# Packed attention and two feed-forward stages on one core: the product with v and the second scores at 128 columns, and one small tile padded to 256 bytes

## The chip, the cores and the metric

The kernel runs on one core of a Trainium2 chip. The metric is the device time of one execution in microseconds (us), and the time before is the median of three executions. One more execution was taken with the hardware profiler; its rows are what the text reads.

## The reference, cut to what matters

```python
p_packed = sm_attn(p, k, v)          # 32 packed queries per head: softmax(p k^T / 8) v
out = sm_attn(q, p_packed, p_packed) # softmax(q p_packed^T / 8) p_packed
x = out as (2304, 512)               # 4 blocks of 576 tokens, 8 heads of 64
x = relu(x @ w_in)**2 @ w_out        # 512 -> 2048 -> 512, weights in float64
logits = x @ w_gate                  # 8 experts; exp, then 8 rounds of row and column balancing give P
out = sum_e P[:, e] * (relu(x @ w1[e]) @ w2[e])   # 512 -> 1024 -> 512
```

## The kernel before, in words

**Attention.** The four blocks b are worked one after the other. Heads go in pairs j = 0..3, a pair filling the 128 partitions (64 each). `scores1(b)` (L191) makes the first scores and their softmax, 128 rows being four heads' 32 packed queries. `pack(b)` (L212) transposes them (`tr`, L219, L224), and multiplies them with v (`pp`, L232): for a pair j and a piece c of the 576 tokens (four of 128, one of 64) the stationary operand is 128 columns of v, the moving one 64 columns of the transposed softmax. Only the two diagonal 64x32 blocks of each 128x64 result are wanted; they are copied into the zeroed tile `bd` (L235 to L238, VectorE the upper half of the partitions, ScalarE the lower). `bd` is also split into two fp32r parts in `BDP` (L243, L244). `scores2(b)` (L250) multiplies 128 tokens of q (stationary) with the 64 columns of `bd` of a pair (`s`, L260), each pair into 64 columns of its own, and takes the softmax on VectorE and ScalarE (L266 to L273). `attn_T` (L276) transposes it (`trc`, `trd`) into `at`.

All these products are in float32. A float32 matmul that is no transpose is issued as two instructions, each with its own weight load, so 20 products of a block are 40 instructions.

**The first feed-forward stage** is built of `g_unit` (L314), which multiplies `BDP` with w_in (L320) and splits the result into the tiles `g` (ACT L329, DVE L330); `h1_unit` (L342), `at` times `g` (L350); and `x2_unit` (L362, L369). Their weights come as float64 words: each piece passes ACT, DVE `cb` (L111) and `cc` (L113), POOL (L114), ACT (L148) and POOL (L149) into a tile `w`, one piece after the other through one buffer `cc`.

**The second feed-forward stage.** Tokens form three groups p of 768, 512 and 1024 tokens (tiles of 384, 256 and 512 columns). `unit(n, p)` (L668) runs seven products of six matmuls each (`product`, L612, matmul L620): stationary are 128 columns of a `w1` tile, moving is a tile `xc` of x. Between the products stand the second matmuls `y_unit` of the unit before (L646: stationary `hh`, moving a `w2` tile). Groups 0 and 1 alternate for n = 0..31; group 2 follows alone for n = 31..62.

**Where the tiles lie.** SBUF tiles come from pools stacked from the left and from the right. The pool `gp` (L500) is opened on the left when attention ends; `xpb`, `wpb`, `gb`, `xca`, `xcb` and `xcc` are opened on top of it. `both` (L503) is `[2 * E, LINE]` floats, 128 bytes in a partition. With it, the tiles of `wpb`, `gb`, `xca`, `xcb`, `xcc` and group 2's `acc` start at 0 modulo 256 bytes in their partition; those of `wpa`, `xc1`, `xcd`, `ta`, `hp` and all of attention's start at 128 modulo 256. A split weight goes to `wpb` if its number k has k % 12 >= 8 (L146, L147), which makes it so that for even n the four `w1` tiles lie in `wpb`, and for odd n in `wpa`; the `w2` tiles lie in `wpa` always. Of group 2's operands B11, B21 and T1 (products A11, A12, S1) lie in `xcc`, the other four (S2, S4, S3, A22) in `ta` and `xcd`.

**The order of work.** The kernel is written block by block, and a scheduler orders the instructions of each engine from that; each engine then works through its own list in order. SP issues the DMAs in order too.

Of the kernel before, what the change touches and what calls it, by code (L numbers as in the profile page):

```python
# [10 lines left out]
F32 = mybir.dt.float32  # L11
F32R = mybir.dt.float32r
I32, U32, I64 = mybir.dt.int32, mybir.dt.uint32, mybir.dt.int64
AF = mybir.ActivationFunctionType
# [7 lines left out]
E, F = 8, 1024  # L22
NJ = H // 2
# [11 lines left out]
LINE = 32  # L35
# [3 lines left out]
def kernel(ctx: ExitStack, tc: tile.TileContext, qT, kT, v, pT,  # L39
                                     win, wout, wg, w1, w2, out):  # L40
    nc = tc.nc

    def open_pool(name, **kw):
        st = ExitStack()
        return st, st.enter_context(tc.tile_pool(name=name, bufs=1, reuse_waits="tile", **kw))

    def pool(name, **kw):
        st, p = open_pool(name, **kw)
        ctx.push(st)
        return p  # L50
# [11 lines left out]
    stA, pa = open_pool("pa", side="left")  # L62
    ps_attn = {}
# [94 lines left out]
    KQ, V = {}, {}  # L158
# [53 lines left out]
    def pack(b, En):  # L212
        vt = V[b]
        ETs = []
        for g in range(2):
            et = pa.tile([128, 5, 128], F32, tag="et", name="et", bufs=2)
            ps = ps_attn["now"].tile([128, 4, 128], F32, tag="tr", name="tr", bufs=3)
            for c in range(4):
                nc.tensor.transpose(ps[:, c, :], En[g][:, c * 128:(c + 1) * 128], ident)  # L219
            nc.scalar.activation(et[:, 0:4, :], ps, AF.Copy)  # L220
            ETs.append(et)
        ps = ps_attn["now"].tile([128, 4, 128], F32, tag="tr", name="tr", bufs=3)
        for g in range(2):
            nc.tensor.transpose(ps[:64, g, :], En[g][:, 512:576], ident)  # L224
        nc.scalar.activation(ETs[0][:64, 4, :], ps[:64, 0, :], AF.Copy)
        nc.scalar.activation(ETs[1][:64, 4, :], ps[:64, 1, :], AF.Copy)
        ps = ps_attn["now"].tile([128, NJ, 64], F32, tag="tr", name="pp", bufs=3)
        for j in range(NJ):
            for c in range(5):
                k = 128 if c < 4 else 64  # L230
                o = j % 2 * 64
                nc.tensor.matmul(ps[:, j, :], vt[:k, c, j * 128:(j + 1) * 128], ETs[j // 2][:k, c, o:o + 64],  # L232
                                 start=(c == 0), stop=(c == 4))

        bd = pa.tile([128, NJ, 64], F32, tag="bd", name="bd", bufs=2)  # L235
        nc.gpsimd.memset(bd, 0.0)
        nc.vector.tensor_copy(bd[0:64, :, 0:32], ps[0:64, :, 0:32])
        nc.scalar.activation(bd[64:128, :, 32:64], ps[64:128, :, 32:64], AF.Copy)  # L238
        bp = BDP[b // 2]
        for par in range(2):  # L240
            o = (par ^ (b % 2)) * 64
            hi, lo, src = bp[:, 0, par::2, o:o + 64], bp[:, 1, par::2, o:o + 64], bd[:, par::2, :]
            nc.scalar.activation(hi, src, AF.Copy)  # L243
            nc.vector.tensor_tensor(lo, src, hi.bitcast(F32), op=ALU.subtract)  # L244
        return bd
# [4 lines left out]
    def scores2(b, bd):  # L250
        a2 = pa.tile([128, 5, H, NP], F32, tag="a2", name="a2", bufs=2)
        for t0 in (0, 2, 4):
            nt = min(2, 5 - t0)
            ps = ps_attn["now"].tile([128, 2, 256], F32, tag="tr", name="s2", bufs=3)
            for t in range(nt):
                o = TOFF[t0 + t]
                for g in range(2):
                    for jj in range(2):
                        at = g * 128 + (jj ^ (b % 2)) * 64
                        nc.tensor.matmul(ps[:, t, at:at + 64], KQ["qt", b, g][:, jj, o:o + 128],  # L260
                                         bd[:, 2 * g + jj, :], start=True, stop=True)
            n = nt * H
            psv = ps[:, :nt, :].rearrange("p t (h c) -> p (t h) c", c=NP)
            a = a2[:, t0:t0 + nt, :, :].rearrange("p t h c -> p (t h) c")
            mx = pa.tile([128, 2 * H, 1], F32, tag="mx2", name="mx2", bufs=2)[:, :n, :]
            nc.vector.tensor_reduce(mx, psv, axis=AX.X, op=ALU.max)  # L266
            nc.vector.tensor_tensor(a, psv, mx.to_broadcast([128, n, NP]), op=ALU.subtract)
            nc.scalar.activation(a, a, AF.Exp, scale=1.0 / np.sqrt(D).item())
            sm = pa.tile([128, 2 * H, 1], F32, tag="sm2", name="sm2", bufs=2)[:, :n, :]
            nc.vector.tensor_reduce(sm, a, axis=AX.X, op=ALU.add)  # L270
            nc.vector.tensor_scalar_add(sm, sm, EPS)
            nc.vector.reciprocal(sm, sm)
            nc.vector.tensor_tensor(a, a, sm.to_broadcast([128, n, NP]), op=ALU.mult)  # L273
        return a2.rearrange("p t h c -> p t (h c)")
# [182 lines left out]
    e0 = scores1(0)  # L457
    e1 = scores1(1)
    bd0 = pack(0, e0)
    load_kq("qt", qT, 1)  # L460
    split_w(2)
    load_kq("kt", kT, 2)
    a0 = scores2(0, bd0)
    bd1 = pack(1, e1)
    load_v(2)
    split_w(2)
# [13 lines left out]
    load_kq("qt", qT, 2)  # L480
    load_kq("kt", kT, 3)
    a1 = scores2(1, bd1)
    e2 = scores1(2)
    moe1(0)
    load_v(3)
    attn_T(1, a1)
    bd2 = pack(2, e2)
    moe1(1)
    load_kq("qt", qT, 3)
    e3 = scores1(3)  # L490
    a2 = scores2(2, bd2)
    bd3 = pack(3, e3)
    attn_T(2, a2)
# [6 lines left out]
    gp = pool("gp", side="left")  # L500
    wgr = gp.tile([128, 4, E], F32, name="wgr")
    wgs = gp.tile([128, 4, 128], F32R, name="wgs")
    both = gp.tile([2 * E, LINE], F32, name="both")[:, :E]  # L503
    nc.vector.tensor_tensor(both, ident[:2 * E, 0:E], ident[:2 * E, E:2 * E], op=ALU.add)
    P = gp.tile([128, 160], F32, name="P")[:, :NT * E].rearrange("p (t e) -> p t e", e=E)
    xpb = pool("xpb", side="left")
# [212 lines left out]
    for n in range(NQ):  # L719
        for p in ROUNDS[0]:  # L720
# [8 lines left out]
            else:  # L729
                k = 2 if p == 0 else 1  # L730
# [60 lines left out]
```

## Time and profile before

| | |
|---|---|
| median of 3 runs | 1968.72 us (1968.06 to 1970.12) |
| the profiled execution | 1963.5 us, span 1961.7 us |
| PE (TensorE) busy | 1940.9 us, 99% |
| PEld (weight loads) busy | 1719.0 us, 88% |
| DVE, ACT, POOL busy | 57%, 41%, 39% |
| chain that ended last | PE 93%, DVE 4% |
| TensorE clock granted | 0.7 of full in the first fortieth of the span, 0.8 in the second, 0.9 or more after |

PE is TensorE's matmuls, PEld its weight loads, DVE VectorE, ACT ScalarE, POOL GpSimd. A row of the timeline gives start, length, engine, line, output<-inputs and the count of merged instructions; in square brackets stands the idle time before it and what ended it. Matmuls overlap, so the spacing of two matmuls is read from starts and not from their length. [...]

### The profile page before, as it was taken

Reading aid. Unit: us, or ns where it says so; the run is one execution under the profiler, and the core shown is the slowest. Engines: PE = TensorE matmul, PEld = TensorE weight load, DVE = VectorE, ACT = ScalarE, POOL = GpSimd, SP = SyncE. Lnnn points to the kernel's source line nnn. Section 1 sums busy time; section 2 is a strip of 40 time slices with the busy share of each in tenths; the row PEclk is TensorE's granted clock in tenths of the full one; section 3 lists DMA queues with packets and bytes.
Section 4 is the critical chain, followed back from the end, with each engine's and each line's share of the span. In section 5 each row is a group of like instructions: output and inputs, shape, how many; then the busy total and the mean of one; then the engine's idle time right before and its main releaser. Section 6 shows DMA issues by size and latency. Waiting matters only on the chain.

```text
span 1961.7 us, 27023 instructions
## 1 busy us (share of the span) xinstructions
PE 1940.9 (99%) x10492; PEld 1719.0 (88%) x10492; DVE 1125.4 (57%) x1959; ACT 806.9 (41%) x1702; POOL 769.5 (39%) x753
## 2 busy tenths in 40 slices
PE   9999999998999999999999999999999999999999
PEld 7899999998989899899999899988888888888887
DVE  4667877655755555555555555663554555555555
ACT  5658654645343333333333333344333333333331
POOL 2204312434433333334334343433544455444550
PEclk7899999999999999999999999999999999999999
DMA  7302201000111101111110110121111111111111
GB/s 262 135 28 87 87 30 36 23 1 33 44 44 44 35 32 43 44 44 43 44 43 33 44 43 34 42 78 52 58 50 43 43 65 54 54 44 43 55 53 43
DMA packets 30496, 103.72 MB, mean 53 GB/s; under 512 B 3360, under 2 KB 3360, under 8 KB 30368
## 3 DMA queue, kind: packets, MB, share of 16 engines
q1 hardware_dynamic: 30368, 102.00, 15.2%
q8 instruction: 82, 1.34, 0.3%
q14 instruction: 46, 0.38, 0.1%
HBM read 97.27 MB, written 4.72 MB: 52 GB/s over the span
## 4 chain that ended last, share of the span: by engine, by line
PE 93%; DVE 4%; ACT 1%; POOL 1%; issue 1%; DMA 0%; SPq 0%; POOLq 0%; ACTq 0%; DVEq 0%
PE psy L646 41%; PE psc L620 36%; PE psy L369 8%; PE psh L350 4%; PE pp L232 1%; DVE h L359 1%; PE s L260 1%; PE psh L320 1%; DVE g L330 1%; PE s L199 1%; DVE cc L113 0%; POOL w L149 0%; POOL cc L114 0%; DVE cb L111 0%; DMA kt<-kT 0%
## 5 line engine op out<-in xcount | busy, mean ns | idle before, releaser
L646 PE MATMUL psy<-w,hh 128*128 128x512 f32 x3456 | 870.5, 392 | 0.0
L646 PEld LDWEIGHTS psy<-w,hh 128*128 128x128 f32 x3456 | 634.0, 188 | 120.8 <-DVE acc L664 1.2
L620 PE MATMUL psc<-xc,w 128*128 128x512 f32 (+2 forms) x3456 | 680.8, 338 | 2.8 <-ACT s L691 2.4
L664 DVE SCALAR_TENSOR_TENSOR acc<-psy,P,acc 128x512 f32<-128x512 f32 x528 | 395.2, 749 | 452.7 <-PE psy L646 449.0
L620 PEld LDWEIGHTS psc<-xc,w 128*128 128x128 f32 x3456 | 577.6, 189 | 80.4 <-ACT s L691 2.6
L149 POOL TENSOR_TENSOR w<-raw,w 128x512 fp32r<-128x512 f32 (+1 forms) x252 | 297.0, 1184 | 449.8 <-ACT w L148 448.3
L148 ACT ACTIVATE w<-raw 128x512 fp32r<-128x512 f32 (+1 forms) x252 | 143.5, 575 | 339.4 <-PE psc L620 206.0
L149 POOL TENSOR_TENSOR w<-wt,w 128x512 fp32r<-128x512 f32 x126 | 163.3, 1303 | 290.6 <-ACT w L148 281.8
L369 PE MATMUL psy<-h,w 128*128 128x288 f32 x1536 | 231.2, 297 | 1.2 <-DVE h L359 0.9
L369 PEld LDWEIGHTS psy<-h,w 128*128 128x128 f32 x1536 | 212.1, 188 | 3.5 <-DVE h L359 2.6
L627 DVE SCALAR_TENSOR_TENSOR hh<-psc,hh 128x256 fp32r<-128x256 f32 (+2 forms) x288 | 154.7, 548 | 23.5 <-ACT hh L626 23.3
L626 ACT ACTIVATE hh<-psc 128x256 fp32r<-128x256 f32 (+2 forms) x288 | 139.5, 485 | 40.6 <-PE psy L646 31.2
L350 PE MATMUL psh<-at,g 128*128 128x288 f32 x768 | 127.1, 298 | 4.5 <-DVE g L330 4.5
L627 DVE SCALAR_TENSOR_TENSOR hh<-s,hh 128x384 fp32r<-128x384 f32 (+1 forms) x96 | 89.9, 936 | 67.9 <-ACT hh L626 67.8
L148 ACT ACTIVATE w<-wt 128x512 fp32r<-128x512 f32 x126 | 79.0, 627 | 110.2 <-PE psc L620 93.1
L350 PEld LDWEIGHTS psh<-at,g 128*128 128x128 f32 x768 | 111.0, 189 | 6.6 <-issue 5.1
L620 PE MATMUL psc<-xt,w 128*128 128x384 f32 x576 | 115.0, 338 | 0.0
L682 ACT ACTIVATE s<-psc 128x384 f32<-128x384 f32 (+1 forms) x96 | 46.7, 488 | 165.3 <-PE psc L620 165.3
L620 PEld LDWEIGHTS psc<-xt,w 128*128 128x128 f32 x576 | 102.5, 188 | 3.4
L125 POOL TENSOR_TENSOR wt<-raw 128x256 f32<-128x256 f32 x63 | 47.3, 750 | 123.1 <-DMA raw<-w 122.2
L626 ACT ACTIVATE hh<-s 128x384 fp32r<-128x384 f32 (+1 forms) x96 | 50.3, 524 | 108.0 <-PE psy L646 107.2
L149 POOL TENSOR_TENSOR w<-cc,w 128x512 fp32r<-128x512 f32 x32 | 41.8, 1307 | 119.2 <-ACT w L148 87.3
(114 smaller groups left out, 1454.3 us busy)
## 6 DMA issues: line engine op xcount, KB each, us to landing
raw<-w SPq DMA_DIRECT2D x126, 512.0 KB, 3.6
raw<-win SPq DMA_DIRECT2D x16, 512.0 KB, 3.8
raw<-wout SPq DMA_DIRECT2D x16, 512.0 KB, 3.8
kt<-kT SPq DMA_DIRECT2D x8, 576.0 KB, 5.8
qt<-qT SPq DMA_DIRECT2D x8, 576.0 KB, 8.6
out<-acc SPq DMA_DIRECT2D x18, 256.0 KB, 2.0
vt<-v SPq DMA_DIRECT2D x4, 1024.0 KB, 9.0
vt<-v SPq DMA_DIRECT2D x4, 128.0 KB, 9.2
```

The source lines that it names most:

```text
L125: nc.gpsimd.tensor_tensor(s1, a21, a22, op=ALU.add)
L148: nc.scalar.activation(w[:, 0, :n], t, AF.Copy)
L149: nc.gpsimd.tensor_tensor(w[:, 1, :n], t, w[:, 0, :n].bitcast(F32), op=ALU.subtract)
L199: nc.tensor.matmul(ps[:, u, :CT], bq[:, 2 * g + jj, :], kt[:, jj, u * CT:(u + 1) * CT], start=(jj == 0), stop=(jj == 1))
L350: nc.tensor.matmul(ps, gw[:, x, m * 128:(m + 1) * 128], at[:, y, g, o:o + CT], start=(i == 0), stop=(i == 5))
L369: nc.tensor.matmul(ps, w[:, x, d * 128:(d + 1) * 128], h[:, y, :], start=(i == 0), stop=(i == 11))
L620: nc.tensor.matmul(ps[:, :N], w[:, u, o + k * 128:o + (k + 1) * 128], x[v][:, k, :], start=(start and k + u + v == 0), stop=(k == 1 and u ...
L626: nc.scalar.activation(h[:, 0, :], src, AF.Relu)
L627: nc.vector.scalar_tensor_tensor(h[:, 1, :], src, 0.0, h[:, 0, :].bitcast(F32), op0=ALU.max, op1=ALU.subtract)
L646: nc.tensor.matmul(ps, h[:, x, o * 128:(o + 1) * 128], w[:, y, :], start=(i == 0), stop=(i == 5))
L664: nc.vector.scalar_tensor_tensor(a, ps, P[:, tt, e:e + 1], a, op0=ALU.mult, op1=ALU.add)
L682: nc.scalar.activation(s12[:, 0, :], X[:, :N], AF.Copy)
```

## The change

The product with v takes all 128 columns of the transposed softmax (two pairs of heads) instead of 64, and `pp` and `bd` are 128 columns wide for a pair. A pair's two wanted blocks are copied to the 64 columns of `bd` that are its own in the second scores, the other 64 stay zero. The second scores multiply with these 128 columns and add the two pairs of a group in PSUM (start at the first, stop at the second), where each pair had 64 columns of its own. The number of matmuls does not change. The copies into `bd` are two on each engine instead of one, half as large. `both` becomes 256 bytes wide, so every tile opened after it on the left lies 128 bytes further: all of `wpb`, `gb`, `xca`, `xcb`, `xcc` now start at 128 modulo 256, as the others do; `P` goes from 128 to 0.

```diff
-        ps = ps_attn["now"].tile([128, NJ, 64], F32, tag="tr", name="pp", bufs=3)
+        ps = ps_attn["now"].tile([128, NJ, 128], F32, tag="tr", name="pp", bufs=3)
...
-                o = j % 2 * 64
-                nc.tensor.matmul(ps[:, j, :], vt[:k, c, j * 128:(j + 1) * 128], ETs[j // 2][:k, c, o:o + 64],
+                nc.tensor.matmul(ps[:, j, :], vt[:k, c, j * 128:(j + 1) * 128], ETs[j // 2][:k, c, :],
...
-        bd = pa.tile([128, NJ, 64], F32, tag="bd", name="bd", bufs=2)
+        bd = pa.tile([128, NJ, 128], F32, tag="bd", name="bd", bufs=2)
         nc.gpsimd.memset(bd, 0.0)
-        nc.vector.tensor_copy(bd[0:64, :, 0:32], ps[0:64, :, 0:32])
-        nc.scalar.activation(bd[64:128, :, 32:64], ps[64:128, :, 32:64], AF.Copy)
+        for par in range(2):
+            pos = par ^ (b % 2)
+            for h2 in range(2):
+                u = bd[h2 * 64:(h2 + 1) * 64, par::2, pos * 64 + h2 * 32:pos * 64 + h2 * 32 + 32]
+                w = ps[h2 * 64:(h2 + 1) * 64, par::2, par * 64 + h2 * 32:par * 64 + h2 * 32 + 32]
+                if h2 == 0:
+                    nc.vector.tensor_copy(u, w)
+                else:
+                    nc.scalar.activation(u, w, AF.Copy)
...
-                        at = g * 128 + (jj ^ (b % 2)) * 64
-                        nc.tensor.matmul(ps[:, t, at:at + 64], KQ["qt", b, g][:, jj, o:o + 128],
-                                         bd[:, 2 * g + jj, :], start=True, stop=True)
+                        nc.tensor.matmul(ps[:, t, g * 128:(g + 1) * 128], KQ["qt", b, g][:, jj, o:o + 128],
+                                         bd[:, 2 * g + jj, :], start=(jj == 0), stop=(jj == 1))
...
-    both = gp.tile([2 * E, LINE], F32, name="both")[:, :E]
+    both = gp.tile([2 * E, 2 * LINE], F32, name="both")[:, :E]
```

The scheduler's lists change in attention and in the first two passes of the first feed-forward stage; after that they are the same but for a few neighbours. Two places matter. On PE, from the second scores of block 1 (`s_602`, then `s_606`) to the first `x2_unit` (`psy`), before:

```order
L260 MATMUL s_638<-bd,qt 128x64
L320 MATMUL psh<-w,bdp_100 128x512 x6
L260 MATMUL s_638<-bd,qt 128x64 x3
L199 MATMUL s_658<-kt,bdq 128x288 x4
L281 MATMUL trc<-ident,a_601 128x128 x4
L350 MATMUL psh<-at_96,g 128x288 x12
L199 MATMUL s_671<-kt,bdq 128x288 x4
L350 MATMUL psh<-at_96,g 128x288 x6
L281 MATMUL trc<-ident,a_601 128x128 x2
L369 MATMUL psy<-h_491,w 128x288
```

and now:

```order
L325 MATMUL psh<-w,bdp_100 128x512 x3
L265 MATMUL s_642<-bd,qt 128x128 x3
L199 MATMUL s_662<-kt,bdq 128x288 x3
L325 MATMUL psh<-w,bdp_100 128x512 x3
L199 MATMUL s_662<-kt,bdq 128x288
L199 MATMUL s_675<-kt,bdq 128x288 x4
L355 MATMUL psh<-at_96,g 128x288 x6
L286 MATMUL trc<-ident,a_605 128x128 x4
L355 MATMUL psh<-at_96,g 128x288 x6
L286 MATMUL trc<-ident,a_605 128x128 x4
L291 MATMUL trd<-ident,a_605 128x128 x2
L199 MATMUL s_994<-kt,bdq 128x288 x4
```

Both halves of the first scores of block 2 (`s_662`, `s_675`) now stand ahead of the first `h1_unit` (`psh<-at`), and all transposes of block 1 (`trc`, `trd`) ahead of the third.

On DVE, the list up to the softmax of block 1's second scores (`mx` is its row maximum), before:

```order
L113 SCALAR_TENSOR_TENSOR cc<-ca,cb 128x512
L111 TENSOR_SCALAR cb<-ca 128x512
L330 TENSOR_TENSOR g<-psh,g 64x512 x2
L113 SCALAR_TENSOR_TENSOR cc<-ca,cb 128x512
L330 TENSOR_TENSOR g<-psh,g 64x512 x2
L111 TENSOR_SCALAR cb<-ca 128x512
L266 TENSOR_REDUCE mx_611<-s_602 128x16
```

and now:

```order
L113 SCALAR_TENSOR_TENSOR cc<-ca,cb 128x512
L335 TENSOR_TENSOR g<-psh,g 64x512
L111 TENSOR_SCALAR cb<-ca 128x512
L335 TENSOR_TENSOR g<-psh,g 64x512 x2
L271 TENSOR_REDUCE mx_615<-s_606 128x16
L335 TENSOR_TENSOR g<-psh,g 64x512
L113 SCALAR_TENSOR_TENSOR cc<-ca,cb 128x512
```

The first maximum of that softmax has moved ahead of weight conversions: of the `cc` steps six stood before it and now four do; from it to the last `g` of the first `g_unit`s the list holds two `cc` and two `cb` as before, and one `g` and three small steps more.

## Rows read from the trace of the kernel before

**Rows 1.** Busy time by stretches (us from the span's start), count in brackets, granted clock
```profile
core 0: us, PE busy (x) PEld busy (x) DVE busy (x) ACT busy (x) POOL busy (x), PEclk, DMA share, GB/s
6.20:15.00 8.80, 8.38 (x37) 6.12 (x36) 2.89 (x7) 4.81 (x12) 0.52 (x1) 1.00 1.03 362
15.00:19.70 4.70, 4.20 (x35) 3.86 (x32) 1.39 (x5) 4.13 (x13) 0.52 (x1) 1.00 1.04 358
19.80:64.10 44.30, 42.03 (x168) 37.47 (x168) 28.03 (x54) 23.68 (x47) 18.65 (x16) 0.50 0.54 182
23.80:32.30 8.50, 8.50 (x40) 8.50 (x41) 6.54 (x13) 4.67 (x9) 3.81 (x3) 0.50 0.96 314
64.20:70.90 6.70, 2.83 (x16) 2.08 (x14) 6.61 (x13) 4.50 (x10) 2.60 (x3) 1.00 0.96 369
71.00:74.30 3.30, 2.79 (x9) 2.54 (x10) 3.30 (x7) 1.96 (x5) 2.20 (x1) 0.50 0.23 93
74.40:95.00 20.60, 20.60 (x146) 19.07 (x144) 10.15 (x28) 12.49 (x30) 0.00 (x0) 1.00 0.24 84
```
**Rows 2.** Timeline of PE in attention
```profile
17.02 5.99 PE L232 MATMUL pp<-et,vt 64*128 64x64 f32 x32 [0.50 <-ACT et L225]
...
37.76 8.23 PE L232 MATMUL pp<-et,vt 64*128 64x64 f32 x32
...
88.83 2.86 PE L232 MATMUL pp<-et,vt 64*128 64x64 f32 x20
...
104.23 2.12 PE L260 MATMUL s<-bd,qt 128*128 128x64 f32 x18
```
**Rows 3.** Instructions of line 455 (whole span): duration min/median/max ns, first and last start
```profile
L455 PE MATMUL warm<-ones x16: 421/421/582, 1.1 to 4.5; 128*128 128x128 f32 x16
```
**Rows 4.** Instructions on tile bd, 20 to 26 us
```profile
L260 PE MATMUL s<-bd,qt x11: 421/421/476, 23.8 to 25.9; 128*128 128x64 f32 x11
L237 DVE COPY bd<-pp x1: 282/282/282, 23.1 to 23.1; 64x128 f32<-64x128 f32 x1
```
**Rows 5.** Timeline of DVE, 55 to 72 us
```profile
58.10 0.68 DVE L266 TENSOR_REDUCE mx<-s 128x16 f32<-128x512 f32 x1
...
61.93 0.41 DVE L111 TENSOR_SCALAR cb<-ca 128x512 int32<-128x512 int32 x1
...
65.07 0.67 DVE L113 SCALAR_TENSOR_TENSOR cc<-ca,cb 128x512 int32<-128x512 int32 x1
...
70.74 0.62 DVE L330 TENSOR_TENSOR g<-psh,g 64x512 fp32r<-64x512 f32 x1
```
**Rows 6.** Waits, 60 to 75 us: total us, times, longest
```profile
PE psh L350 <- DVE g L330: 4.5, 2, 2.3
```
**Rows 7.** Timeline of PE in group 2: odd n until 1617, then even n
```profile
1602.94 1.52 PE L620 MATMUL psc<-xc,w 128*128 128x512 f32 x6
1604.30 2.88 PE L646 MATMUL psy<-w,hh 128*128 128x512 f32 x12
1607.02 2.92 PE L620 MATMUL psc<-xc,w 128*128 128x512 f32 x12
1609.77 2.90 PE L646 MATMUL psy<-w,hh 128*128 128x512 f32 x12
...
1624.79 1.56 PE L620 MATMUL psc<-xc,w 128*128 128x512 f32 x6
1626.19 1.53 PE L646 MATMUL psy<-w,hh 128*128 128x512 f32 x6
1627.56 1.53 PE L620 MATMUL psc<-xc,w 128*128 128x512 f32 x6
1628.93 1.53 PE L646 MATMUL psy<-w,hh 128*128 128x512 f32 x6
```
**Rows 8.** Timeline of PE in group 0: even n at 918, odd n at 945
```profile
918.72 2.29 PE L620 MATMUL psc<-xt,w 128*128 128x384 f32 x12
920.85 1.55 PE L646 MATMUL psy<-w,hh 128*128 128x512 f32 x6
...
945.05 2.27 PE L620 MATMUL psc<-xt,w 128*128 128x384 f32 x12
947.16 2.92 PE L646 MATMUL psy<-w,hh 128*128 128x512 f32 x12
```

More of the change, by code (lines that the diff above doesn't have):

```diff
@@ L241, in pack @@
             o = (par ^ (b % 2)) * 64
-            hi, lo, src = bp[:, 0, par::2, o:o + 64], bp[:, 1, par::2, o:o + 64], bd[:, par::2, :]
+            hi, lo, src = bp[:, 0, par::2, o:o + 64], bp[:, 1, par::2, o:o + 64], bd[:, par::2, o:o + 64]
             nc.scalar.activation(hi, src, AF.Copy)
```

## The prediction

> **What bounds the kernel now.** The page says PE: 99% busy and 93% of the chain that ended last. A busy PE can still be a slow one, so the view by stretches comes first [rows 1]. [...] In the long low stretch PE is busy 42.03 of 44.30 us: it works at half speed and is the bound. From 64.2 to 70.9 us PE is busy 2.83 us only and DVE 6.61 of 6.70 us: there DVE is the bound, and the waits name it, the `h1_unit` matmuls waiting 4.5 us for `g` [rows 6]. From 74.4 us PE is busy all the time at the high level [rows 1]. So 55 us near the start are worth looking at, and the remaining 1890 us are worth what one matmul costs.
>
> **What the engine did when its clock changed.** Before the fall it streamed the 64-column products with v and waited in between: 4.20 us busy of 4.70 [rows 1], a record of busy time that the columns do not enter. It then streamed 64-column second scores without a gap, 8.50 of 8.50 us, and the clock stayed low [rows 1]. In the stretch from 6.2 us with products of 288 columns it stayed high [rows 1]. Narrow products thus keep the engine formally busy without bringing the clock back; that the wide ones would is a conclusion from these stretches and not shown in them.
>
> **The change, part by part. Width.** 320 instructions go from 64 to 128 columns (two products of 20 matmuls in four blocks, two instructions each). At the low level a 64-column one takes (25.9 - 23.8) / 10 = 0.21 us [rows 4]. The warm-up matmuls had 128 columns and the same 421 ns as those at the low level, and they stand (4.5 - 1.1) / 15 = 0.23 us apart with their start-up [rows 3, 4]. So the second 64 columns cost 0 to 0.02 us at the low level: the loading of 128 stationary columns sets the pace and the stream hides behind it. At the high level 64 columns take (2.12 - 0.27) / 17 = 0.11 us [rows 2]; no row has two-pass products of 128 columns there, and I carry the zero over. The exception is where 64-row and 128-row pieces of v alternate: 20 instructions with eight such changes take (2.86 - 0.27) / 19 = 0.136 us each [rows 2], so a change costs about 0.067 us more, which looks like load and stream one after the other. Wider streams can at most double that: 64 changes by 0.067 us is 4.3 us, the least is 0. The copies into `bd` become two on DVE and two on ACT, of half the 0.28 us each at best [rows 4], with the second scores waiting for the first pair only; 0 to 0.3 us for each of four blocks. I take 1.5 us for all of this, nearer the lower end since it holds for all but the changes.
>
> [...]
>
> **Clock.** If the wide products hold the clock up, the 42.03 us of PE work in the low stretch shrink by at most half, 21 us [rows 1]. Only part of it arrives, because DVE and ACT do not get faster. Step by step: the first product with v resumed at 17.02 us and ended at 23.0 us [rows 2]; 32 instructions at 0.136 us end it at 21.5 us. The second scores began 0.8 us later [rows 4] and their 40 instructions end at about 27 us instead of 32.3 us. The rest of the next product with v ran from 37.76 to 46.0 us [rows 2]; its start waits for softmax, transposes and copies that keep their times but for ten transposes and eight pairs at half speed (about 1.7 us), so it starts about 7 us earlier and takes 4.4 instead of 8.2 us: 10.8 us earlier at its end. From there to the row maximum at 58.10 us [rows 5] are 12.1 us; the new list puts two conversions (0.41 + 0.67 us each [rows 5]) and one `g` (0.62 us [rows 5]) behind it, so this piece loses 2.8 us. From the maximum to the end of the last `g` (71.36 us [rows 5]) DVE hardly pauses; 13.3 us become 14.5 us with that `g` and small steps. Together 10.8 + 2.8 - 1.2 = 12.4 us, taken as 12, earlier at the point where PE stops waiting for DVE. The other 9 of the 21 us turn into longer waits for DVE.
>
> Those waits have a price. PE had 6.70 us with little to do before, and the clock was low for the 3.3 us after it, 2.79 us of work at half speed, about 1.4 us lost [rows 1]. The wait now is longer, some 8 us, and I add 2.5 us for one or two more low stretches (0 to 5). In the new PE list the last transposes of block 1 stand ahead of the third `h1_unit`; they wait for DVE, up to about 2 us, but first scores of block 3 are pulled ahead as well, so I count nothing. The weight conversions now two places later are wanted by `x2_unit` several us after; they are covered by the same DVE wait, and cost their 2.2 us of DVE in the stretch after 74.4 us, where DVE is busy 10.15 of 20.60 us [rows 1]. On SP, first-score loads of block 2 now stand ahead of one weight load, waiting for the second scores of block 0, which end 5 us earlier: nothing. Attention: -12 + 2.5 + 1.5 = **-8 us** (0 to -13).
>
> **Padding.** The same product in group 2 takes different times. Six matmuls of 512 columns take 1.36 us from start to start with both operands at 128 modulo 256 (1602.94 to 1604.30), 1.40 us with weights at 0 and x at 128 (1624.79 to 1626.19), and 1.37 us with both at 0 (1627.56 to 1628.93); twelve, half of them with weights at 128 and x at 0, take 2.75 us (1607.02 to 1609.77), 1.36 + 1.39 [rows 7]. So unequal places cost 0.03 to 0.04 us a product, whichever operand is the odd one. Afterwards all lie at 128. For even n: four products at 0.04 and three at 0.01 us, 0.19 us; for odd n three at 0.03 us, 0.09 us; sixteen of each: 4.5 us. In group 0 twelve matmuls of 384 columns take 2.13 us for even n and 2.11 us for odd [rows 8], 0.01 us a product; fourteen products, sixteen even n: 2.2 us (0 to 4.5, as the rows round). Together **-6.7 us** (0 to -9).
>
> [...]
>
> **Sum.** -8 - 6.7 = -14.7 us on the profiled 1963.5 us, 1948.8 us. The median of the runs is 5.2 us above that execution; I put the change on the median: 1968.72 - 14.7 = **1954.0 us**.
>
> **Rivals.**
> *The padding brings nothing,* and only the clock counts: 1968.7 - 8 = 1960.7 us. For it: the spread between places is 3% of a product and might follow something else that alternates with n. Against it: its sign turns with x's place within the same n [rows 7]. [...]
> *The clock falls as before,* so that the width does not do what it is for: the drop at 19.8 us may come from the wait in front of it, and PE still waits there. Attention then keeps its time, 1968.7 - 6.7 = 1962 us. Against it: the back-to-back stretch that stayed low [rows 1] has 64 columns throughout.
> *The columns are paid for in full:* if 128 columns cost twice the 0.11 us of 64 at the high level, 320 instructions add 35 us, half of which would be too much: slower as soon as an instruction grows by more than 14.7 / 320 = 0.046 us. With the clock gain and the padding kept it gives 1968.7 + 35 - 14.7 = 1989 us. Against it stand the equal durations at the low level [rows 3, 4]. [...]
>
> **How the numbers follow.** Forecast, both gains: 0.63. Padding nothing: 0.17. Clock as before: 0.12. Columns paid: 0.05. The remaining 0.03 is a schedule that loses its gain to DVE. The range takes the bounds of both gains nearly in full downwards, 1968.7 - 13 - 9 = 1946.7, so 1946 us, and the first two rivals upwards: 1946 to 1963 us. Within 0.2% (3.9 us), about what a measurement can tell from no change, is 1964.8 to 1972.6 us: small remainders of the first two rivals, 0.08. Slower by more: the third and part of the rest, 0.06. Faster: 0.86.
>
> **What would show it.** Right: a granted clock of 1.00 from 19.8 us on to the wait for `g`, in the view by stretches; 128-column instructions 0.11 us apart; the first product with v ending near 21.5 us, the next near 36 us; the last `g` near 59 us; and every six-matmul product of group 2 at 1.36 us. Wrong: a clock at 0.50 through the second scores, a pair above 0.15 us, or group 2 products still at 1.40 us.

## The result and the profile after

The changed kernel takes **1942.38 us** (median of 4 runs, 1940.22 to 1942.72), the kernel before 1968.39 us in the same comparison (4 runs, 1968.03 to 1970.12): a ratio of 0.9864, 95% interval 0.9847 to 0.9881. The forecast was 1954.0 us, with a range from 1946. The sign and both mechanisms came out as forecast, the gain was 26.0 us instead of 14.7, and the time lies below the range.

| | before | after |
|---|---|---|
| the profiled execution | 1963.5 us, span 1961.7 | 1940.2 us, span 1938.3 |
| PE busy | 1940.9 us | 1915.8 us |
| mean granted clock | 0.988 | 0.997 |
| chain that ended last | PE 93%, DVE 4% | PE 94%, DVE 4% |

The clock comes first. The view by stretches of the changed kernel, in the stretches of [rows 1] (PEclk, the third figure from the end, is the granted clock as a share of full speed; [rows 1] hold two levels of it, 1.00 and 0.50, and a value between them is a mean over the stretch):

```profile
19.80:64.10 44.30, 35.36 (x220) 30.39 (x219) 39.49 (x82) 31.22 (x66) 20.58 (x17) 0.92 0.70 245
23.80:32.30 8.50, 7.59 (x61) 6.81 (x61) 8.43 (x18) 6.07 (x13) 4.92 (x5) 1.00 1.03 367
64.20:70.90 6.70, 6.70 (x48) 6.00 (x47) 5.47 (x15) 6.70 (x18) 2.94 (x3) 1.00 0.52 170
71.00:74.30 3.30, 3.30 (x24) 2.92 (x24) 1.77 (x5) 2.13 (x7) 0.00 (x0) 1.00 0.71 230
74.40:95.00 20.60, 20.60 (x163) 20.12 (x162) 11.74 (x33) 10.09 (x26) 0.53 (x1) 1.00 0.22 74
```

From 19.8 to 64.1 us PE is less busy (35.36 against 42.03 us) and starts more (220 matmuls against 168): the clock is 0.92 instead of 0.50 [rows 1]. The long low stretch is one of 6.8 us, 52.4 to 59.2 us by the trace's clock record. In the stretches 64.2 to 70.9 us and 71.0 to 74.3 us, where PE waited and then ran at half clock before, it is busy all the time at 1.00 (6.70 of 6.70 and 3.30 of 3.30 us).

PE's timeline in attention, which answers to [rows 2]:

```profile
16.43 5.00 PE L231 MATMUL pp<-et,vt 64*128 64x128 f32 x32 [0.45 <-ACT et L225]
22.05 4.87 PE L265 MATMUL s<-bd,qt 128*128 128x128 f32 x40 [0.63 <-ACT bd L244]
...
28.81 6.19 PE L231 MATMUL pp<-et,vt 128*128 128x128 f32 x40
...
47.42 0.65 PE L199 MATMUL s<-kt,bdq 128*128 128x288 f32 x2
53.30 4.21 PE L199 MATMUL s<-kt,bdq 128*128 128x288 f32 x8 [5.22 <-ACT e L205]
56.89 2.06 PE L355 MATMUL psh<-at,g 128*128 128x288 f32 x6
58.74 0.82 PE L286 MATMUL trc<-ident,a 128*128 128x128 f32 x4
59.32 1.04 PE L355 MATMUL psh<-at,g 128*128 128x288 f32 x6
```

The two products with v end at 21.4 and 35.0 us (23.0 and 46.0 before). The 40 wide instructions of the second scores stand (4.87 - 0.27) / 39 = 0.118 us apart, those of the product (6.19 - 0.27) / 39 = 0.152 us. The long wait of PE is now in front of the second half of the first scores of block 2, 5.22 us for the exponential (`e`), and the low stretch begins in it. On DVE [rows 5]:

```profile
43.71 0.69 DVE L271 TENSOR_REDUCE mx<-s 128x16 f32<-128x512 f32 x1
...
56.51 0.68 DVE L335 TENSOR_TENSOR g<-psh,g 64x512 fp32r<-64x512 f32 x1
```

The maximum comes 14.4 us earlier than before, the last `g` ends at 57.2 us, 14.2 us earlier. In group 2, an even n [rows 7]:

```profile
1582.44 1.52 PE L625 MATMUL psc<-xc,w 128*128 128x512 f32 x6
1583.80 2.88 PE L651 MATMUL psy<-w,hh 128*128 128x512 f32 x12
1586.52 2.88 PE L625 MATMUL psc<-xc,w 128*128 128x512 f32 x12
1589.24 2.88 PE L651 MATMUL psy<-w,hh 128*128 128x512 f32 x12
```

Six matmuls take 1.36 us and twelve 2.72 us, where an even n had 1.40 and 1.37.

Where the time went, by the start of one matmul of each place in the traces (us from the span's start; "columns" is experiment e1, the change without the padding):

| start of | before | columns | after |
|---|---|---|---|
| last matmul of the second product with v | 45.58 | 34.71 | 34.73 |
| first `h1_unit` | 68.15 | 56.85 | 56.89 |
| seventh `h1_unit` matmul, behind the last `g` | 71.51 | 59.15 | 59.32 |
| second feed-forward stage | 447.80 | 431.81 | 431.88 |
| group 2 | 1281.50 | 1266.39 | 1264.17 |
| last matmul | 1957.47 | 1942.50 | 1934.06 |

The columns gain 15.0 us and the padding 8.4 us, 23.4 in all; the medians lie 26.0 apart because the profiled execution of before was 4.9 us below its median in this comparison and that of after 2.2 us.

### The profile page after: what moved, and what is told of

It is laid out like the page before. It is cut to its first block, busy times and chain, and to the rows that moved or that the text cites. A ratio compares the mean times of both kernels' runs of the same rounds, so it can differ in the third digit from the quotient of the medians.

```text
span 1938.3 us, 27038 instructions
## 1 busy us (share of the span) xinstructions
PE 1915.8 (99%) x10492; PEld 1700.7 (88%) x10492; DVE 1122.7 (58%) x1963; ACT 805.6 (42%) x1706; POOL 771.2 (40%) x753
## 3 DMA queue, kind: packets, MB, share of 16 engines
q1 hardware_dynamic: 30368, 102.00, 15.6%
## 4 chain that ended last, share of the span: by engine, by line
PE 94%; DVE 4%; ACT 1%; issue 0%; POOL 0%; DMA 0%; POOLq 0%; ACTq 0%; DVEq 0%
PE psy L651 41%; PE psc L625 36%; PE psy L374 9%; PE psh L355 4%; PE pp L231 1%; DVE h L364 1%; PE psh L325 1%; DVE g L335 1%; PE s L199 1%; DVE cc L113 0%; PE s L265 0%; DVE cb L111 0%; PE psy L431 0%; DVE x L382 0%; DVE s L362 0%
## 5 line engine op out<-in xcount | busy, mean ns | idle before, releaser
L125 POOL TENSOR_TENSOR wt<-raw 128x256 f32<-128x256 f32 x63 | 47.2, 749 | 124.1 <-DMA raw<-w 123.5
```

The costliest lines, as they stand in the source:

```text
L125: nc.gpsimd.tensor_tensor(s1, a21, a22, op=ALU.add)
```

## The experiments

All kernels were timed beside the kernel before, whose median was 1968.3 us in the comparisons of e1 to e8 and 1969.8 in that of e9 and e10.

**e1, the columns alone** (the change with `both` as before):

```diff
-    both = gp.tile([2 * E, 2 * LINE], F32, name="both")[:, :E]
+    both = gp.tile([2 * E, LINE], F32, name="both")[:, :E]
```

> The change without the padding. Theory (two independent gains, the larger from the clock): the second feed-forward stage keeps the spacing of before, group 2 pairs of units 41.19 us, and the time falls by the attention part, 15.9 us in the profiled pair of before and after, to 1950 to 1953 us by the median; the clock is high from 6 us to some 52 us. Rival (the width is worth little, the padding carries most): above 1960 us.

Measured: 1949.84 us (6 runs, 1948.49 to 1951.00), ratio 0.9911 (0.9892 to 0.9929), 0.2 us below the expected range. The clock, 1.00 from 19.8 to 48.9 us and 0.78 from there to 64.1 us in both traces, and the start times are those of the whole change until the second stage: the clock belongs to the columns.

**e2, the padding alone** (the kernel before with the other line of e1's diff).

> The padding alone, attention as before. Theory (a matmul is slower when its moving operand and the next weight load lie at different places modulo 256 bytes): attention and the low clock from 19.8 to 64.1 us stay, group 2 products at 1.36 us each, and the time falls by 8.4 us, which is what the second stage lost between the two profiles, to 1959 to 1961 us. [...]

Measured: 1957.81 us (6 runs, 1954.92 to 1961.86), 0.9951 (0.9932 to 0.9970), 1.2 us below the expected range. In the traces, group 2 takes 669.8 us from its first matmul to the last one, 669.9 in the whole change, 676.0 in the kernel before and 676.1 in e1. Groups 0 and 1 take 832.1 and 832.3 us with padding, 833.7 and 834.6 without. So -6.2 and about -2 us belong to the padding; the median fell by more, for the runs of this kernel and of the one before differ in their clock (below). Attention is as before in kind, with more low stretches in the profiled execution:

```profile
19.80:64.10 44.30, 36.95 (x171) 31.68 (x170) 28.45 (x54) 23.86 (x48) 18.82 (x16) 0.65 0.55 184
64.20:70.90 6.70, 2.41 (x10) 1.88 (x10) 6.61 (x13) 4.53 (x9) 2.55 (x2) 0.64 0.98 371
...
95.00:131.00 36.00, 36.00 (x251) 34.62 (x251) 17.74 (x46) 16.08 (x42) 0.53 (x1) 0.91 0.17 51
```

**e3, the product with v alone, and e4, the second scores alone.** e3 keeps 64 columns in `bd` and copies from the wide `pp`; e4 keeps `pp` narrow:

```diff
 e3
+                nc.tensor.matmul(ps[:, j, :], vt[:k, c, j * 128:(j + 1) * 128], ETs[j // 2][:k, c, :],
...
                         nc.tensor.matmul(ps[:, t, at:at + 64], KQ["qt", b, g][:, jj, o:o + 128],
 e4
                 nc.tensor.matmul(ps[:, j, :], vt[:k, c, j * 128:(j + 1) * 128], ETs[j // 2][:k, c, o:o + 64],
...
+                        nc.tensor.matmul(ps[:, t, g * 128:(g + 1) * 128], KQ["qt", b, g][:, jj, o:o + 128],
```

> Only the product with v at 128 columns; the second scores stay at 64 columns, padding as before. Theory (the columns streamed keep the clock up): the clock does not fall at 19.8 us but after the first second scores, at 64 columns for 4.5 us, and is low for part of the stretch to 64 us; time 1955 to 1966 us. Rival (it is the wait in front of the products that drops the clock): it falls at about 19.8 us all the same and the time is within 2 us of before.

> Only the second scores at 128 columns; the product with v stays at 64 columns, padding as before. Theory (columns streamed): the clock falls at about 19.8 us as before, in the narrow product, and rises during or right after the first second scores; time 1952 to 1962 us. Rival (the scheduler's new order carries the gain and the width none): clock low until 64 us.

Measured: e3 1951.85 us (4 runs), 0.9919 (0.9897 to 0.9941); e4 1953.42 us (4 runs), 0.9928 (0.9907 to 0.9949). e3's view by stretches, and PE's timeline with its second scores at 64 columns:

```profile
19.80:64.10 44.30, 36.50 (x215) 30.97 (x215) 36.37 (x79) 30.24 (x62) 18.40 (x16) 0.88 0.68 234
```
```profile
22.79 4.82 PE L260 MATMUL s<-bd,qt 128*128 128x64 f32 x40 [0.63 <-ACT bd L238]
```

The same two views of e4, with its product with v at 64:

```profile
19.80:64.10 44.30, 36.12 (x193) 30.44 (x193) 36.12 (x73) 27.65 (x55) 19.42 (x16) 0.75 0.68 229
```
```profile
16.47 6.70 PE L232 MATMUL pp<-et,vt 64*128 64x64 f32 x32 [0.50 <-ACT et L225]
23.80 7.04 PE L266 MATMUL s<-bd,qt 128*128 128x128 f32 x40 [0.63 <-ACT bd L245]
```

In e4 the clock falls in the narrow product (low from 18.4 to 28.7 us), rises in the wide scores, falls again in the next narrow product (38.9 to 45.7). In e3 it falls behind the narrow scores, for 3.4 us only (29.5 to 32.9). Each expectation had the order of falls and rises right; e4's time lies in its range, e3's gain of 16.4 us was larger than expected. The two rows of second scores also tell what the columns cost while the clock is high: 40 instructions take 4.82 us with 64 columns (e3, 22.79) and 4.87 us with 128 (the whole change, 22.05). The two gains, 16.4 and 14.9 us, don't add: together they are 18.5, since each half already spares much of the same low stretch.

**e5, unequal places everywhere, and e6, equal places at another value.**

```diff
 e5
     const = pool("const", side="left")
+    const.tile([128, 32], F32, name="shift")
 e6, in addition
-    edge.tile([128, 24], F32, name="edge")
+    edge.tile([128, 56], F32, name="edge")
```

> The changed kernel with 32 floats more at the start of the left side of SBUF: every tile of the left side (both weight pools, the first xc0) then begins at 0 modulo 256 bytes, every tile of the right side (hh, xc1, xt) stays at 128; the order of instructions is the same on every engine. Theory (a matmul is slower where its moving rows and the next matmul's stationary rows differ by 128 modulo 256 bytes): the 2954 pairs in which one second product follows another (w at 0 moving, hh at 128 stationary next) go from 227 to about 232.5 ns, about +16; the 1162 pairs of 512 columns in the first products of group 2 the same, about +6; pairs of 256, 384 and 288 columns +1 to +4: 1942.4 + 25 = about 1967 (1962 to 1972). Rival (the padding gains by something else, such as the place of one tile): within 2 us of the changed kernel, 1940 to 1945.

> As e5, and the right side shifted by 32 floats as well, so that weights, xc and hh all begin at 0 modulo 256 bytes: the offsets agree again, at another value. Theory (only the agreement counts): the pairs of 512 columns stand at 227 to 228 ns, 1941 to 1947. Rival (128 is a good place and 0 a bad one, or any move costs): as slow as e5 or between, 1950 to 1970.

Measured: e5 1958.59 us (6 runs), e6 1941.77 us (4 runs), the whole change 1942.38. Equal places at 0 are as good as at 128, unequal ones cost 16.8 us with the same order of instructions: what counts is whether the two sides agree. e5's timeline in group 2:

```profile
1616.39 1.55 PE L652 MATMUL psy<-w,hh 128*128 128x512 f32 x6
1617.78 1.56 PE L626 MATMUL psc<-xc,w 128*128 128x512 f32 x6
1619.17 1.56 PE L652 MATMUL psy<-w,hh 128*128 128x512 f32 x6
1620.57 1.55 PE L626 MATMUL psc<-xc,w 128*128 128x512 f32 x6
1621.96 1.56 PE L652 MATMUL psy<-w,hh 128*128 128x512 f32 x6
```

Every six take 1.39 to 1.40 us here, where they took 1.36 in the whole change. The time is below the expected 1962 to 1972 us. The expectation was 25 us because it took all 2954 pairs of second products at 227 ns. In group 2 they do go from 226.7 to 232.9 ns (mean of start to start at the high clock), but in groups 0 and 1 they stand at 231.1 ns with equal places already and go to 232.1 only; group 2 accounts for 15.6 us, groups 0 and 1 for 3.1 between the two traces.

**e7, narrow columns with added matmuls.** The kernel before, and in blocks 0 and 1:

```diff
+            if b < 2:
+                nc.tensor.matmul(ps[:, NJ:, :].rearrange("p j c -> p (j c)"), vt[:, 0, j * 128:(j + 1) * 128],
+                                 ETs[j // 2][:, 0:2, :].rearrange("p c n -> p (c n)"), start=True, stop=True)
...
+                if b < 2:
+                    nc.tensor.matmul(ps[:, t, :], KQ["qt", b, 0][:, 0, o:o + 128],
+                                     bd.rearrange("p j c -> p (j c)"), start=True, stop=True)
```

> The kernel before, with its narrow columns and without the padding, and in blocks 0 and 1 one more matmul of 256 columns (its result is overwritten or unread) behind every five of the product with v and ahead of every four of the second scores: more work, none of it needed. Theory (the wide columns gain only because they hold the clock): the granted clock stays at 1.00 through 19.8:32.3 and nearly to the wait, as in the kernel with the columns alone, and against that kernel's 1949.8 the narrow instructions give back about 3 and the added ones cost about 4: 1948 to 1954. Rival (the clock falls for the weight loads or for a wait and not for the narrow columns, or the columns gain otherwise): clock 0.5 from about 19.8 on, and the added 18 x 2 instructions of each block cost 4 to 9 on top of the kernel before: 1970 to 1978.

Measured: 1962.79 us (10 runs, 1957.13 to 1975.51), 0.9979 (0.9960 to 0.9999), between the two expectations. In the profiled execution the clock holds through the product and the scores of block 0 and falls at 34.7 us, 15 us later than before, in the product of block 1:

```profile
16.63 0.70 PE L235 MATMUL pp<-et,vt 128*128 128x256 f32 x2
17.16 1.36 PE L232 MATMUL pp<-et,vt 128*128 128x64 f32 x10
...
24.93 0.65 PE L262 MATMUL s<-bd,qt 128*128 128x256 f32 x2
25.42 1.00 PE L267 MATMUL s<-bd,qt 128*128 128x64 f32 x8
...
35.44 2.42 PE L232 MATMUL pp<-et,vt 128*128 128x64 f32 x10
37.80 1.22 PE L235 MATMUL pp<-et,vt 128*128 128x256 f32 x2
...
67.38 1.06 PE L357 MATMUL psh<-at,g 128*128 128x288 f32 x6
69.75 2.21 PE L199 MATMUL s<-kt,bdq 128*128 128x288 f32 x8 [1.31 <-ACT e L205]
```

An added matmul takes 17.16 - 16.63 = 0.53 us in the product and 25.42 - 24.93 = 0.49 us in the scores, so that 18 of them are some 9 us and not the 4 of the expectation. The runs themselves show what the clock is worth. With the low level at 0.50 [rows 1], the time at it, estimated from the mean granted clock of a run, is 2 x (1 - clock) x span:

| e7, one run | mean clock | low, us |
|---|---|---|
| 1957.13 us | 0.998 | 8 |
| 1959.65 us | 0.997 | 12 |
| 1963.48 us | 0.993 | 27 |
| 1969.45 us | 0.990 | 39 |
| 1975.51 us | 0.985 | 59 |

One kernel, one order of instructions: 51 us more at the low level go with 18.4 us more time. In its three fastest runs, where the clock held best, the kernel before with some 9 us of unneeded work was 8 to 11 us below the kernel before's median, and 1.7 to 4.6 us below that kernel's fastest run in the same comparison (1961.72 us). Over all ten runs the gain is 0.2%. e1's 1949.8, plus 9 for the added matmuls, less 1 to 2 for the narrow columns, is 1957 to 1958, near the fastest run. That run also bears on a rival, that the scheduler's new order carries e1's gain: e7 keeps the order of before where it matters, the second half of the first scores of block 2 (69.75) behind twelve `h1_unit` matmuls. The new order was not run by itself. The kernel before shows the worth of the clock too: in the comparison of e1 to e4 it took 1962.81 us in a run at 0.989 and 1972.02 us in one at 0.983, 24 us of low clock and 9.2 us.

**e8, 128 columns in blocks 0 and 1 alone, and e10, the same once more.**

```diff
+                r, q = (ps[:, j, :], ETs[j // 2][:k, c, :]) if b < 2 else (ps[:, j, o:o + 64], ETs[j // 2][:k, c, o:o + 64])
...
+                        if b < 2:
+                            nc.tensor.matmul(ps[:, t, g * 128:(g + 1) * 128], KQ["qt", b, g][:, jj, o:o + 128],
+                                             bd[:, 2 * g + jj, :], start=(jj == 0), stop=(jj == 1))
+                        else:
+                            nc.tensor.matmul(ps[:, t, g * 128 + at:g * 128 + at + 64], KQ["qt", b, g][:, jj, o:o + 128],
+                                             bd[:, 2 * g + jj, at:at + 64], start=True, stop=True)
```

> The changed kernel with 128 columns in blocks 0 and 1 alone; blocks 2 and 3 go back to 64 columns (copies and padding stay). Theory (in blocks 2 and 3 the clock is held by the matmuls of the feed-forward stage that are mixed in, and wide columns only cost their own length): 80 instructions of the product 0.016 us and 80 of the scores 0.007 us shorter, about -1.9: 1939 to 1942. Rival (the clock falls in blocks 2 or 3 as it did in the first): a low-clock stretch between 75 and 450 us and 1944 to 1955.

> The kernel of e8 once more, unchanged, beside e9 on one chip: 1937 to 1940 in each run, and about 3 us less than the changed kernel's 1940 to 1943 (theory of e8); if e8's gain was the spread of runs, 1940 to 1944.

Measured: 1938.88 us (4 runs, 1937.12 to 1939.13), 0.9857 (0.9836 to 0.9879), and 1936.34 us (4 runs, 1935.85 to 1938.88), 0.9838 (0.9820 to 0.9857). Both are below what was expected, e8 by 0.1 us, e10 in three runs of four by 0.6 to 1.2 us. No run of the two is above 1939.13, and none of the whole change is below 1940.22, though the whole change was not timed again beside them. In e8's profiled execution the first `h1_unit` starts at 56.87 us as in the whole change, the second stage at 429.17 instead of 431.88. The clock stays at 1.00 through the narrow columns of blocks 2 and 3 (64.2 to 131 us); the low stretch from 428.7 to 432.1 us is at the start of the second stage, where the whole change has one at 458.6. Here the wide columns only cost, but little: by the spacing of starts, the 160 instructions of the two blocks take 18.7 us in e8 and 19.7 us in the whole change, 1.0 of the 2.7 us. Another 1.0 us is the low stretch, which ends at 56.6 us in e8 and at 59.2 us in the whole change, so that no `h1_unit` runs in it, and 0.4 us is idle time.

**e9, the wait filled.** e8 with eight more matmuls in the wait of 5.2 us:

```diff
+            if b == 2 and g == 1:
+                fill = ps_attn["now"].tile([128, 256], F32, tag="tr", name="fill", bufs=3)
+                for _ in range(8):
+                    nc.tensor.matmul(fill, ident, KQ["kt", b, 0][:, 0, 0:256], start=True, stop=True)
```

> The kernel of e8 (128 columns in blocks 0 and 1 alone) with eight more matmuls of 256 columns, whose result nobody reads, between the two groups of the first scores of block 2, where TensorE waits 5.2 us for the exponential and then runs at 0.50 (52.4 to 59.2 in the changed kernel, 52.4 to 55.8 in e8). One of them took 0.53 us in e7, so they fill 4.2 of the 5.2. Theory (a low stretch follows an idle stretch, and costs half of the work that stands in it): the clock stays at 1.00 over 48.9:64.1 and the first scores behind the wait and the first matmuls of the feed-forward stage end 1 to 2.5 us earlier: 1 to 2.5 us below e8. Rival (what ends the wait and the last g on DVE decide, not TensorE): the clock stays up and the time does not move, within 0.5 of e8. Second rival: the added matmuls run past the end of the wait and cost up to 2.

Measured: 1938.44 us (5 runs, 1936.56 to 1938.74), 0.9846 (0.9829 to 0.9864), within 0.5 us of e8 and 2.1 us above e10, whose runs overlap with its own: no faster. e9's timeline:

```profile
48.12 3.62 PE L199 MATMUL fill<-kt,ident 128*128 128x256 f32 x16
53.50 2.21 PE L203 MATMUL s<-kt,bdq 128*128 128x288 f32 x8 [1.77 <-ACT e L209]
55.33 1.17 PE L365 MATMUL psh<-at,g 128*128 128x288 f32 x6
...
57.46 1.06 PE L365 MATMUL psh<-at,g 128*128 128x288 f32 x6 [0.53 <-DVE g L345]
...
59.77 2.02 PE L365 MATMUL psh<-at,g 128*128 128x288 f32 x12 [0.80 <-DVE s L372]
```

The clock held to 427.9 us, the scores took 2.21 us instead of 3.73 in e8 (4.21 in the whole change), the first `h1_unit` started 1.5 us earlier than in e8, and then PE waited for DVE's `g` and `s`. By the second stage 1.1 us were left, within the spread of the runs. So this low stretch, beside a late DVE, was worth little.

## Why the prediction fell short

**The steps of the clock came out, the last of them by luck.** The change holds the granted clock at 1.00 through the second scores and to the wait (until 52.4 us). The forecast put the end of the first product with v at 21.5 us (measured 21.4), of the second near 36, 35.2 by its own sum (35.0), the last `g` near 59 (57.2). "12 us earlier at the point where PE stops waiting for DVE" measured 71.51 - 59.15 = 12.4 us [rows 5, 6], but two errors cancel in it. The last `g` came 14.2 us earlier, not 12.4, and PE did not wait for it any more. PE's long wait was 5.2 us for the exponential, where the prediction had "some 8 us" for DVE. Behind it eight first scores and six `h1_unit` matmuls ran at half clock without a gap, and PE reached its seventh `h1_unit` matmul some 2 us after `g` was ready (59.32 against 57.19).

**The step that failed is what follows it: "-12 + 2.5 + 1.5".** Four us were to be given back behind the wait; instead 3.6 more were gained by the start of the second stage, and 1.0 was given back in that stage, 15.0 us in all. From the seventh `h1_unit` matmul to the second stage, in the kernel before and in e1:

```profile
71.51:447.80 376.29, 371.52 (x2697) 361.15 (x2697) 265.54 (x556) 225.18 (x529) 113.83 (x102) 1.00 0.14 44
```
```profile
59.15:431.81 372.66, 368.45 (x2691) 358.28 (x2690) 264.70 (x555) 226.06 (x535) 117.70 (x106) 1.00 0.15 47
```

The stretch is 3.6 us shorter: 3.1 us less busy and 0.6 us less idle. The work that stood at its start in the kernel before:

```profile
62.67 2.89 PE L199 MATMUL s<-kt,bdq 128*128 128x288 f32 x8
...
71.51 1.78 PE L350 MATMUL psh<-at,g 128*128 128x288 f32 x6 [2.33 <-DVE g L330]
73.09 2.75 PE L199 MATMUL s<-kt,bdq 128*128 128x288 f32 x8
```

Summed by the spacing of starts, three terms of the prediction went another way. (1) "Some 2.5 us for one or two more low stretches": the old low stretch behind the wait, which the prediction priced at 1.4 us, was left in the sum as if it stayed. It is gone, and the `h1_unit` matmuls take 0.9 us less for it. The new one, 52.4 to 59.2 us, lies ahead of the seventh `h1_unit` matmul and is inside the 12.4. One more, 458.2 to 461.7 us in e1, lies in the second stage, where 0.9 of the 1.0 us were given back within the first 42 us. (2) The first scores of block 2 had no term. Eight of their instructions moved from 73.09 us to a place ahead of the `h1_unit`: 2.1 us less behind it, and a part of why PE came 2 us after `g` ahead of it. (3) The columns, 1.5 us for all four blocks, were added behind the wait; the half of them that lies there costs 0.6 us. The `x2_unit` matmuls take 0.8 us less and the transposes 0.1 us more. Why these do was not found. The idle time is shorter by the waits for `h` (0.6 against 0.9 us) and for `at` (1.7 against 1.9 us).

**The price of the columns came out.** While the clock is high, instructions of the scores follow each other at 0.112 us with 64 columns and with 128, and so do those of the product between two pieces of 128 rows of v. The weight loads are busy nearly all the time in both: 1.87 of 1.87 us in narrow scores (before, 104.23 to 106.10), 4.58 of 4.65 us in the wide ones (after, 22.05 to 26.70). At a piece of 64 rows two spacings of each pair of heads grow from 0.160 to 0.213 us, 0.11 us a pair and 1.7 us for all sixteen. The mean of 0.152 us in the product comes from these pieces, whose spacings were 0.16 to 0.21 us with 64 columns too; that it lies above the 0.15 us named as a sign of being wrong is mostly their doing and not that of the width. The rival that added 35 us had the price some twenty times too high.

**The padding was undersized: 8.4 us instead of 6.7.** Group 2 gave 6.1 us where 4.5 stood. Its products gave 4.4 of them, about what the prediction had from rows read to 0.01 us. The second matmuls gave the other 1.7; the prediction counted none, though one that is followed by a `w1` tile at 0 took 232.4 ns against 226.8. Groups 0 and 1 gave 1.6 (e2) to 2.3 us (from e1 to the whole change) where 2.2 stood. The rival "the padding brings nothing" is refuted by e5 and e6: 1958.59 us with unequal places, 1941.77 us with equal ones at 0.

**The rest is the reference point.** The profiled execution of before had less low clock than most runs (mean 0.988; the median run of e1's comparison 0.984). The prediction put its sum, made on that execution, unchanged on the median; but the runs of before vary with their low clock (two of them under e7), and the change removes most of it: its own runs lie within 2.5 us. That is 2.7 us of the miss, beside 7.0 in attention and 1.7 in the padding.

## What to carry to other kernels

A PE that is shown busy may be at half clock (here 42.03 of 44.30 us busy at 0.50 [rows 1]): read the granted clock by stretches, and where it is low beside narrow matmuls, try them with columns that cost no time (here 0.112 us an instruction with 64 and with 128), but only there (e8). If the stretches of low clock differ from run to run, compare the clock of the profiled execution with that of the median run: a change that removes them can gain another amount on each (here 23.4 us between the traces and 26.0 between the medians). When a wait moves, take what hung on its old place out of the sum, not only put in what hangs on the new one. A low stretch beside a late engine was worth little here (e9: the scores took 2.21 us instead of 3.73, and the median stayed within 0.5 us of e8's).

## What the runs showed of the hardware

- The spacing of 512-column matmuls in group 2 went with the places of the moving and the stationary operands modulo 256 bytes: 226.7 (after) to 227.5 ns (second matmuls before) where both lie at 128, 226 to 227 ns within a product where both lie at 0 (before, the four from 1627.79 us), and 232 to 233 ns, on the mean of six, where one lies at 0 and the other at 128 (before, e5). Whether a matmul's own stationary operand or that of the next one counts is not settled: before the change, for even n, the last second matmul ahead of a product (its own operands at 128, the next weights at 0) took 232.4 ns, and the last matmul of a product with x at 128 and weights at 0 ahead of `hh` at 128 took 232.5 ns. In groups 0 and 1 agreement is not enough: second matmuls there take 231 ns with all places equal. In e5 every six took 1.39 to 1.40 us, also products that agree at 0 between matmuls that don't; why was not tried, nor were shifts of less than 128 bytes.
- Two-instruction float32 matmuls on 128 rows follow each other at 112 ns with 64 (before) and with 128 columns (after) at clock 1.00, and at 213 ns with either at 0.50 (before, e3 and e4).
- 64-column matmuls without a gap, 8.50 us busy of 8.50, left the clock at 0.50 [rows 1], and one wide product of the two kept it up from 5.6 to 53.4 us but for 3.4 us (e3).
- In e2 and e7 the clock also fell near 120 us (120.7 to 127.5 and 116.6 to 123.5), in e8 with the same narrow columns there it did not. What differs, and why runs of the kernel before vary in this, stays open.
